# Attention feeding a hard-swish MLP: head-pair tokens in 128 by 3 plus shared blocks of 64, in place of 112 by 4

## The chip, the cores and the metric

The kernel runs on one core of a Trainium2 chip. The metric is device time in microseconds (us), the median of several runs of the whole program. The engines are TensorE (PE in the profile, with its weight loads as PEld), VectorE (DVE), ScalarE (ACT), GpSimd (POOL) and SyncE (SP). SP issues nearly all the DMAs.

## The reference

Two parts, one after the other. All inputs and the output are float32.

```python
# q, k, v: (8 batches, 12 heads, 448 tokens, 64); g_q, g_k: (64,)
def rmsnorm(x, g):
    return x / np.sqrt(np.mean(x * x, axis=-1, keepdims=True) + 1e-06) * g
q_n, k_n = rmsnorm(q, g_q), rmsnorm(k, g_k)
scores = q_n @ k_n.T / sqrt(64)              # per batch and head, 448 x 448
attn = softmax(scores)                       # the row maximum is subtracted first
a = attn @ v
x = a, as (8 * 448, 12 * 64)                 # 3584 x 768
h = x @ w_in                                 # w_in 768 x 2048
g = h * clip(h + 3, 0, 6) / 6
out = g @ w_out                              # w_out 2048 x 768, out 3584 x 768
```

## The kernel before

The work unit of attention is the head pair, two heads of one batch. There are 48 of them, P = 0 to 47, six per batch. The 448 tokens of a head pair are mapped as 112 partitions by T = 4, token p * 4 + t. For each head pair:

- `load` (L376) issues three DMAs on SP: q, k and v of both heads, 224 KB each, in rows of 1 KB.
- `prep` (L388) squares q and k on ACT or POOL, sums the squares per token on VectorE (L406), takes ln and exp on ACT (L411, L414) for the reciprocal root, multiplies q and k by it into bfloat16 `qks` (L423, POOL, and VectorE for the first head pair), and casts v into `va` (L345, L347, L351), which has a column of ones beside each 64 values.
- `trans` (L446) turns `qks` so that the two heads' 64 features lie on 128 partitions and tokens run along the free axis: the tile `T`, 448 columns of queries and 448 of keys. For the first 13 head pairs TensorE transposes (L475) and VectorE or ACT copies; from the 14th on it is a DMA transpose on SP (L451). The keys take the gains and the scale along (L460, L462, L484, L486).
- `score` (L498) multiplies, for a block t of keys, each head's 64 feature rows with all 448 queries. The two heads use the upper and the lower 64 rows of TensorE side by side (L506). ACT takes the exponential of both heads at once, 896 columns, from PSUM to `eT` (L515). No maximum is subtracted, since the normed scores are bounded.
- `av` (L520) uses `eT` as the stationary operand, 128 columns of queries at a time, and streams the 65 columns of `va` (L527): 8 matmuls per key block, 32 per head pair, summed over the four blocks in the PSUM tile `X`. The 65th column is the softmax sum.
- `finish` (L533) takes the reciprocal of the sums (L539), multiplies (L542) and turns the result into `xT`, features on partitions: by TensorE for batches 0 and 1 (L558), by DMA transpose from batch 2 on (L549).

The MLP works per batch: `h_group` (L567) makes 128 of the 2048 hidden features for 448 tokens in six matmuls (L579), ACT makes the clamp's lower half (L586, a Relu with 1/6 folded in), and VectorE does the upper half and the product with h into `gT` (L589). `y_group` (L597) makes 128 tokens of the output for a pair of batches, 2 x 16 matmuls of 384 columns (L610), copied by ACT or VectorE (L347, L349) and stored by one to several DMAs, since a block of 128 tokens cuts the 112-partition map at changing places. The weights are loaded and cast to bfloat16 by four DMAs each on POOL's queue (L645, L650).

The order is written out. Every step is an operation of a `Plan` with reads, writes and a wished time; the list `ORDER` gives the sequence of all operations, and each engine executes its own in that sequence. The table `WAY` names the operations that use the second or third of several possible engines. So each engine's queue is fixed, and an engine waits at the head of its queue. PSUM is divided into two score tiles S, one tile X for AV (and for some scores) and two banks M for the MLP. Head pairs are grouped for scores: one key block at a time for the first six, two at a time to head pair 23, and from 24 on three blocks (the third in X) with the fourth joined to the first of the next head pair. MLP matmuls lie between these groups.

Of the kernel before, what the change touches and what calls it, by code (L numbers as in the profile page):

```python
# [8 lines left out]
FP32 = mybir.dt.float32  # L9
# [3 lines left out]
A_MIN = mybir.AluOpType.min  # L13
LN = mybir.ActivationFunctionType.Ln
# [7 lines left out]
WAY = {53: 1, 63: 2, 67: 1, 68: 1, 69: 1, 78: 1, 83: 1, 84: 1, 95: 1, 101: 1, 126: 1, 132: 2, 157: 1,  # L22
    163: 1, 183: 1, 188: 1, 225: 1, 231: 1, 233: 1, 245: 1, 250: 1, 256: 1, 276: 1, 358: 1, 365: 1, 377: 1,
    388: 1, 400: 1, 424: 2, 429: 1, 446: 1, 453: 1, 458: 1, 460: 1, 487: 1, 500: 1, 505: 1, 516: 1, 518: 1,
    533: 1, 625: 1, 636: 1, 676: 1, 683: 2, 709: 2, 714: 1, 728: 1, 729: 1, 755: 1, 761: 2, 766: 1, 793: 1,
    798: 1, 821: 1, 892: 1, 899: 2, 925: 2, 930: 1, 945: 1, 951: 2, 977: 2, 1003: 2, 1008: 1, 1023: 1,
    1029: 1, 1034: 1, 1061: 1, 1097: 1, 1134: 1, 1148: 1, 1182: 2, 1206: 1, 1212: 1, 1226: 1, 1251: 1,
    1257: 2, 1263: 1, 1398: 1, 1413: 1, 1420: 2, 1426: 1, 1440: 1, 1447: 1, 1453: 1, 1464: 1, 1465: 1,
    1491: 1, 1515: 1, 1516: 1, 1522: 1, 1549: 1, 1555: 1, 1579: 1, 1615: 1, 1620: 1, 1652: 1, 1673: 1,
    1693: 1, 1700: 1, 1706: 1, 1718: 1, 1724: 2, 1744: 1, 1751: 2, 1757: 1, 1781: 1, 1795: 1, 1832: 1,  # L30
    1893: 1, 1921: 1, 1932: 1, 1938: 1, 1958: 1, 1971: 1, 1979: 1, 1980: 1, 1986: 1, 1992: 1, 2057: 1,
    2062: 1, 2093: 1, 2098: 1, 2125: 1, 2145: 1, 2162: 1, 2169: 1}


class Plan:
# [51 lines left out]
    8, 9, 20, 13, 21, 22, 15, 23, 11, 24, 28, 10, 25, 19, 29, 53, 26, 12, 30, 27, 14, 54, 31, 16, 55, 32, 33,  # L87
    34, 17, 58, 35, 56, 36, 83, 37, 92, 38, 78, 59, 39, 60, 40, 57, 62, 41, 18, 69, 42, 43, 44, 61, 45, 93,
    68, 66, 46, 73, 47, 67, 64, 123, 48, 101, 70, 49, 50, 74, 122, 65, 75, 71, 63, 77, 104, 72, 217, 102, 84,
    105, 76, 81, 85, 154, 51, 103, 112, 94, 124, 82, 79, 52, 86, 114, 80, 113, 153, 126, 115, 110, 87, 95,  # L90
    155, 135, 88, 111, 96, 91, 89, 136, 106, 116, 184, 117, 107, 133, 97, 118, 90, 143, 119, 185, 156, 108,
    134, 132, 120, 186, 144, 109, 141, 121, 248, 142, 145, 146, 166, 98, 1, 157, 164, 147, 167, 158, 148, 99,
    165, 174, 163, 149, 215, 137, 150, 159, 172, 100, 125, 387, 138, 151, 175, 127, 0, 139, 216, 173, 218,
    140, 187, 152, 195, 128, 197, 188, 129, 196, 176, 177, 178, 198, 130, 179, 189, 203, 160, 204, 205, 131,
    246, 180, 168, 181, 190, 206, 161, 169, 170, 247, 182, 171, 191, 183, 162, 228, 385, 226, 229, 207, 194,
    208, 386, 201, 227, 199, 192, 209, 416, 202, 210, 200, 236, 211, 234, 225, 212, 237, 230, 414, 219, 213,
    249, 259, 214, 231, 6, 220, 238, 260, 239, 193, 235, 445, 267, 2, 221, 232, 240, 222, 268, 241, 257, 223,
    242, 233, 243, 415, 258, 250, 261, 244, 262, 245, 265, 256, 251, 277, 266, 278, 224, 269, 279, 280, 281,
# [109 lines left out]
def kernel(  # L208
# [11 lines left out]
    nc = tc.nc  # L220

    B, H, S, D = q.shape
    DM, DFF = moe_w_in.shape
    NPAIR = H // 2
    NP = B * NPAIR
    T = 4
    TP = S // T
    NKT = DM // 128
    NFT = DFF // 128
    E1 = D + 1  # L230
    HALF = DM // 2
    S2 = 2 * S
# [58 lines left out]
    for t in va_r:  # L291
        nc.gpsimd.memset(t[:, :, :, D:E1], 1.0)
# [481 lines left out]
```

## Time and profile before

| | |
|---|---|
| time, median of 3 runs | 432.89 us (431.69 to 434.04) |
| the profiled execution | 432.39 us |
| its span, first to last instruction | 430.6 us |
| TensorE busy | 415.5 us, 97% of the span |
| ACT busy | 296.6 us, 69% |
| VectorE busy | 220.7 us, 51% |
| POOL busy | 171.8 us, 40% |
| mean granted TensorE clock | 0.988 |
| DMA packets | 94418, of which 53156 under 512 bytes |
| HBM read, written | 45.61 MB, 11.01 MB |

The profile is one execution. In its forty slices each digit is the busy share in tenths of a slice of 10.8 us. In groups and in the timeline a line names the line of the kernel, the engine, the operation, the tile written and those read, the shape and the count. A matmul's duration includes its way through the array, so matmuls in a row overlap and start-to-start distances give their price. In a list of waits the numbers are total us, times and the longest one.

### The profile page before, as it was taken

How to read it: one execution, taken by the hardware profiler on the slowest of the kernel's cores; microseconds unless marked ns; L12 is line 12 of the kernel's file. 1: busy time of each engine (PE TensorE's matmuls, PEld its weight loads, DVE VectorE, ACT ScalarE, POOL GpSimd, SP SyncE). 2: the span in 40 equal slices, each digit the busy share in tenths (PEclk: the TensorE clock that was granted, in tenths of full speed). 3: DMA queues.
4: the chain of work that ended last, by engine and by line, in shares of the span. 5: the costliest groups of instructions: out<-in, count | busy, mean ns of one | idle time of the engine just before them, and what ended most of it. 6: DMA issues, size and time to landing. Idle time of an engine off the chain costs nothing.

```text
span 430.6 us, 9771 instructions
## 1 busy us (share of the span) xinstructions
PE 415.5 (97%) x3874; PEld 238.0 (55%) x3874; DVE 220.7 (51%) x405; ACT 296.6 (69%) x535; POOL 171.8 (40%) x188
## 2 busy tenths in 40 slices
PE   7678999999999999999999999999999999999996
PEld 7445555555555555555555555555555555655554
DVE  5665677557688865565556344434424332143211
ACT  4988899898998888968856978575575546222221
POOL 2897865876647867345434350312200000000000
PEclk9968999999999999999999999999999999999999
DMA  8999999499979999657564755262313221021113
GB/s 211 257 246 253 238 241 248 103 227 219 223 203 216 208 220 231 177 145 184 149 158 118 202 147 130 65 117 70 78 32 84 49 59 49 12 73 38 37 39 110
DMA packets 94418, 63.13 MB, mean 147 GB/s; under 512 B 53156, under 2 KB 90916, under 8 KB 94372
## 3 DMA queue, kind: packets, MB, share of 16 engines
q1 hardware_dynamic: 88736, 55.88, 53.5%
q0 software_dynamic: 5248, 6.29, 8.3%
q8 instruction: 30, 0.49, 0.5%
q10 hardware_dynamic: 388, 0.34, 0.3%
q14 instruction: 16, 0.13, 0.1%
HBM read 45.61 MB, written 11.01 MB: 132 GB/s over the span
## 4 chain that ended last, share of the span: by engine, by line
PE 90%; DMA 5%; ACT 2%; DVE 1%; issue 1%; SPq 1%
PE M L579 32%; PE M L610 29%; PE X L527 11%; PE S L506 9%; PE S L610 5%; DMA qk<-in_q_dram 3%; DMA vf<-in_v_dram 2%; PE X L579 1%; ACT eT L515 1%; PE X L506 1%; PE S L579 1%; PE X L610 1%; DVE ssq L406 1%; SPq L384 1%; DVE gT L589 0%
## 5 line engine op out<-in xcount | busy, mean ns | idle before, releaser
L515 ACT ACTIVATE eT<-S 112x896 bf16<-112x896 f32 x168 | 148.0, 918 | 16.1 <-PE S L506 15.6
L579 PE MATMUL M<-xT,w_in_sb 128*128 128x448 bf16 x714 | 153.2, 353 | 0.6 <-ACT xT L347 0.3
L610 PE MATMUL M<-w_out_sb,gT 128*128 128x384 bf16 x752 | 135.9, 326 | 0.0
L589 DVE SCALAR_TENSOR_TENSOR gT<-ts,M 128x448 bf16<-128x448 f32 x119 | 73.4, 619 | 102.6 <-ACT ts L586 102.4
L423 POOL TENSOR_TENSOR qks<-qk,rs 112x512 bf16<-112x512 f32 x94 | 96.2, 1044 | 61.8 <-DMA T<-qks 33.5
L610 PEld LDWEIGHTS <-gT 128*128 128x128 bf16 x912 | 84.8, 98 | 62.1 <-issue 9.9
L586 ACT ACTIVATE ts<-M 128x448 f32<-128x448 f32 x119 | 64.8, 547 | 61.4 <-PE M L579 60.2
L579 PEld LDWEIGHTS <-w_in_sb 128*128 128x128 bf16 x768 | 69.9, 98 | 65.4 <-issue 10.8
L399 POOL TENSOR_TENSOR sq<-qk 112x512 f32<-112x512 f32 x56 | 57.7, 1040 | 44.8 <-DMA qk<-in_k_dram 18.3
L527 PEld LDWEIGHTS <-eT 112*128 112x128 bf16 x1536 | 57.8, 99 | 19.0 <-issue 8.7
L406 DVE TENSOR_REDUCE ssq<-sq 112x16 f32<-112x1024 f32 (+1 forms) x50 | 58.0, 1172 | 15.9 <-ACT sq L397 11.6
L527 PE MATMUL X<-va,eT 112*128 112x65 bf16 x1536 | 62.8, 196 | 1.0 <-DVE xT L349 0.6
L506 PE MATMUL S<-T 64*128 64x448 bf16 x336 | 48.5, 363 | 4.2 <-ACT eT L515 2.1
L542 DVE TENSOR_TENSOR xn<-X,rd 112x512 bf16<-112x512 f32 x48 | 33.2, 691 | 1.8 <-DVE rd L539 0.2
L351 POOL CAST va<-vf 112x512 bf16<-112x512 f32 x20 | 12.8, 638 | 45.3 <-PE X L527 42.8
L506 PEld LDWEIGHTS <-T 64*128 64x128 bf16 x384 | 13.1, 94 | 29.8 <-issue 22.5
L397 ACT ACTIVATE sq<-qk 112x512 f32<-112x512 f32 x40 | 24.8, 627 | 4.6 <-DMA qk<-in_k_dram 3.1
L347 ACT COPY y<-M 128x384 f32<-128x384 f32 x26 | 12.5, 481 | 18.7 <-PE M L610 18.4
L539 DVE RECIPROCAL rd<-X 112x8 f32<-112x8 f32 x48 | 9.8, 204 | 30.1 <-PE X L527 29.8
L349 DVE COPY y<-M 128x384 f32<-128x384 f32 x21 | 11.7, 555 | 22.8 <-PE M L610 22.6
L515 ACT ACTIVATE eT<-X 112x896 bf16<-112x896 f32 x24 | 22.1, 923 | 0.0
L610 PE MATMUL S<-w_out_sb,gT 128*128 128x384 bf16 (+1 forms) x128 | 21.8, 316 | 0.0
(56 smaller groups left out, 178.6 us busy)
## 6 DMA issues: line engine op xcount, KB each, us to landing
qk<-in_q_dram SPq DMA_DIRECT2D x48, 224.0 KB, 4.4
qk<-in_k_dram SPq DMA_DIRECT2D x48, 224.0 KB, 3.9
vf<-in_v_dram SPq DMA_DIRECT2D x48, 224.0 KB, 4.4
w_in_sb<-in_moe_w_in_dram POOLq DMA_DIRECT2D x4, 768.0 KB, 14.5
w_out_sb<-in_moe_w_out_dram POOLq DMA_DIRECT2D x4, 768.0 KB, 15.1
out_dram<-y SPq DMA_DIRECT2D x7, 336.0 KB, 2.8
out_dram<-y SPq DMA_DIRECT2D x8, 288.0 KB, 2.7
out_dram<-y SPq DMA_DIRECT2D x8, 240.0 KB, 2.8
```

What stands on the lines that cost most here:

```text
L397: em(nc.scalar.square(out=sq[:, i], in_=x))
L399: em(nc.gpsimd.tensor_tensor(out=sq[:, i], in0=x, in1=x, op=A_MULT))
L406: em(nc.vector.tensor_reduce(out=ssq[:, s].rearrange("p i n -> p (i n)"), in_=sq[:, s].rearrange("p i (n d) -> p (i n) d", d=D), axis=AX_X ...
L423: em((nc.vector if e == DVE else nc.gpsimd).tensor_tensor(out=qks[:, i].rearrange("p t h d -> p h t d"), in0=qk[:, i].rearrange("p h (t d) ...
L506: em(nc.tensor.matmul(out=ps[:, a, 0:S], lhsT=qkT[r, S + t * TP:S + t * TP + 128], rhs=qkT[r, 0:S], start=True, stop=True))
L515: em(nc.scalar.activation(out=eT[:, t, 0:S2].rearrange("p (a s) -> p a s", a=2), in_=ps[0:TP, :, 0:S], func=EXP, bias=0.0, scale=1.0))
L527: em(nc.tensor.matmul(out=X_ps[:, a, i * E1:(i + 1) * E1], lhsT=eT[:, t, c:c + 128], rhs=va[:, a, t, :], start=(t == 0 and i == 0), stop=( ...
L542: em(nc.vector.tensor_tensor(out=xn[:].rearrange("p i a d -> p a i d"), in0=xv[:, :, :, 0:D], in1=rd[:].unsqueeze(3).to_broadcast([TP, 2, ...
L579: em(nc.tensor.matmul(out=ps[:, 0:S], lhsT=w_in_sb[:, kt, f * 128:(f + 1) * 128], rhs=xT[:, kt, :], start=(kt == 0), stop=(kt == NKT - 1)))
L586: em(nc.scalar.activation(out=ts[:], in_=ps[:, 0:S], func=RELU, bias=0.5, scale=1.0 / 6.0))
L589: em(nc.vector.scalar_tensor_tensor(out=gT[:, f, e * S:(e + 1) * S], in0=ts[:], scalar=1.0, in1=ps[:, 0:S], op0=A_MIN, op1=A_MULT))
L610: em(nc.tensor.matmul(out=ps[:, 0:nc0], lhsT=gT[:, f, i * 128:(i + 1) * 128], rhs=w_out_sb[:, f, c0:c0 + nc0], start=(f == 0), stop=(f == ...
```

## The change

The token map becomes 128 partitions by 3, token p * 3 + t, for the first 384 tokens of a head, and the last 64 tokens (RT) are in blocks of their own, shared by the head pairs 2m and 2m+1:

- The last 64 queries of the even and the odd head pair share one block of 128 columns, so that in `T`, which now holds two head pairs, the even one's 448 queries end where the odd one's begin.
- The last 64 keys of a head pair's two heads lie on a diagonal: head 0 in rows 0 to 63 and columns 0 to 63, head 1 in the others, zeros elsewhere. One matmul over all 128 rows gives both heads' scores for them, with keys of head 0 on partitions 0 to 63 and of head 1 on 64 to 127 (`rest`). Its exponential has 448 columns for both heads.
- The values of these keys lie on a diagonal too, `vb`, 130 columns: one AV matmul serves both heads.

Per head pair there are three key blocks with 896-column exponentials and one of 448; 24 AV matmuls of 65 columns and 4 of 130. Loads are three DMAs of 192 KB per head pair, in rows of 768 bytes, and per two head pairs six of 32 KB in rows of 256 bytes. `prep` scales q and k on POOL or, in the first batch, on VectorE in six instructions of one 64-element group each. The DMA transposes have nine blocks of 128 for the even head pair and six for the odd, in place of eight of 112 for each.

Two things change beside. The clamp of the MLP can run on ACT (Relu of h + 3) or on VectorE (h held between -3 and 3), with the other half in the product and the sixth in the output copy. The score groups are one key block at a time to head pair 5, two and one to head pair 17, then three at once; no group joins two head pairs. `ORDER` and `WAY` are new throughout. The core of the diff:

```diff
-    T = 4
-    TP = S // T
+    T = 3
+    TP = 128
+    RT = S - T * TP
...
+    KE, KR, QE, QR, QO, KO = 0, 3 * TP, 5 * TP, 8 * TP, 9 * TP, 12 * TP
...
-    NQK, NV, NSQ, NRS, NQS, NVA, NT, NE, NXN, NXT, NTS, NY = 5, 5, 2, 4, 3, 4, 4, 2, 2, 2, 2, 3
+    NQK, NV, NVR, NSQ, NRS, NQS, NVA, NVB, NT, NE, NXN, NXT, NTS, NY = 5, 5, 2, 2, 4, 2, 4, 3, 2, 2, 2, 2, 2, 3
...
-    qks_r = ring(NQS, [TP, 2, T, 2, D], BF16, "qks")
-    va_r = ring(NVA, [TP, 2, T, E1], BF16, "va")
-    T_r = ring(NT, [128, S2 + PAD], BF16, "T")
-    eT_r = ring(NE, [TP, T, S2 + PAD], BF16, "eT")
+    qke_r = ring(NQS, [TP, 9, 2, D], BF16, "qke")
+    qko_r = ring(NQS, [TP, 6, 2, D], BF16, "qko")
+    va_r = ring(NVA, [TP, 2 * T, E1], BF16, "va")
+    vb_r = ring(NVB, [TP, 2, 2, E1], BF16, "vb")
+    T_r = ring(NT, [128, 15 * TP], BF16, "T")
+    eT_r = ring(NE, [TP, T, S2 + 2 * PAD], BF16, "eT")
+    eR_r = ring(NE, [TP, S + 2 * PAD], BF16, "eR")
...
+            for n in range(2):
+                r = slice(n * RT, n * RT + RT)
+                if c == "R":
+                    rows = src[b, four, T * TP:S, :].rearrange("(o h) r d -> o r h d", o=2)[n]
+                    dst = qk[r, FULL + 2 * D:FULL + 4 * D].rearrange("p (h d) -> p h d", h=2)
+                else:
+                    rows = src[b, four, T * TP:S, :].rearrange("(o h) r d -> h r o d", o=2)[n]
...
+                if e == DVE:
+                    for h in range(2):
+                        for t in range(T):
+                            c = c0 + h * T + t
+                            em(nc.vector.tensor_scalar(
+                                qks[:, b0 + t, h], x[:, h, t], rs[:, c:c + 1], None, A_MULT, A_ADD,
+                                accum_out=junk_t[:]))
...
+    def rest(P, want):
+        ps, res = sbank()
+
+        def f_sr(_):
+            qkT, k0, q0 = T_r[P // 2 % NT], KR + P % 2 * TP, queries(P)
+            em(nc.tensor.matmul(
+                out=ps[:, 0, 0:S], lhsT=qkT[:, k0:k0 + TP], rhs=qkT[:, q0:q0 + S], start=True, stop=True))
+
+        def f_er(_):
+            em(nc.scalar.activation(
+                out=eR_r[P % NE][:, PAD:PAD + S], in_=ps[:, 0, 0:S], func=EXP, bias=0.0, scale=1.0))
+        plan.add(pe(0.19), want, f_sr, sorted(treads(P, ["KR"])), [res])
+        plan.add([act(S)], want, f_er, [res], [("e", P % NE, T)])
...
         def f_av(_):
-            for a in range(2):
-                for i in range(T):
-                    c = a * S + i * TP
+            for i, c in enumerate(columns(P)):
+                for h in range(2 if t < T else 1):
+                    c0 = PAD + h * S + c
+                    o = (i % 2 * 2 + h) * E1
                     em(nc.tensor.matmul(
-                        out=X_ps[:, a, i * E1:(i + 1) * E1], lhsT=eT[:, t, c:c + 128],
-                        rhs=va[:, a, t, :], start=(t == 0 and i == 0), stop=(t == T - 1),
-                        skip_group_check=True))
+                        out=X_ps[:, i // 2, o:o + (E1 if t < T else 2 * E1)],
+                        lhsT=eT[:, t, c0:c0 + TP] if t < T else eR[:, c0:c0 + TP],
+                        rhs=va[:, h * T + t, :] if t < T else vb[:, P % 2].rearrange("p h e -> p (h e)"),
+                        start=(t == 0 and h == 0 and i % 2 == 0), stop=(t == T), skip_group_check=True))
...
-        def f_r(_):
-            em(nc.scalar.activation(out=ts[:], in_=ps[:, 0:S], func=RELU, bias=0.5, scale=1.0 / 6.0))
+        def f_r(eng):
+            made_by.append(eng)
+            if eng == ACT:
+                em(nc.scalar.activation(out=ts[:], in_=ps[:, 0:S], func=RELU, bias=3.0, scale=1.0))
+            else:
+                em(nc.vector.tensor_scalar(ts[:], ps[:, 0:S], -3.0, 3.0, A_MAX, A_MIN))
...
-        plan.add([act(S)], want + dt, f_r, [res], [("ts", key)])
+        plan.add([act(S), dve(S)], want + dt, f_r, [res], [("ts", key)])
...
-        if P < NPAIR:
+        if P < NG0:
             groups = [([(P, t, False)], w + t * step) for t in range(T)]
...
-            groups = [([(P, t, False), (P, t + 1, False)], w + t * step) for t in (0, 2)]
+            groups = [([(P, 0, False), (P, 1, False)], w), ([(P, 2, False)], w + 2 * step)]
...
-        elif P % 2 == 0:
-            groups = [([(P, 0, False), (P, 1, False), (P, 2, True)], w),
-                      ([(P, 3, False), (P + 1, 0, False)], w + G2 * step)]
-            aw, fw = w + AE * step, w + FE * step
-        else:
-            groups = [([(P, 1, False), (P, 2, False), (P, 3, True)], w + G3 * step)]
-            aw, fw = w + AO * step, w + FO * step
+        else:
+            groups = [([(P, 0, False), (P, 1, False), (P, 2, True)], w)]
+            aw, fw = w + AE * step, w + FE * step
```

## The prediction, made before the changed kernel was run

> **What bounds the kernel now.** The page came first: its busy times, then the forty slices.
>
> ```profile
> PE 415.5 (97%) x3874; PEld 238.0 (55%) x3874; DVE 220.7 (51%) x405; ACT 296.6 (69%) x535; POOL 171.8 (40%) x188
> ...
> PE   7678999999999999999999999999999999999996
> ...
> ACT  4988899898998888968856978575575546222221
> ...
> PEclk9968999999999999999999999999999999999999
> DMA  8999999499979999657564755262313221021113
> ```
>
> TensorE is the engine that is never free, except in the first four slices (43 us). There the clock drops too (6 and 8 tenths), ACT runs at 8 to 9 tenths and the DMA engines at 8 to 9. So there are two kernels in one: a start-up paced by ACT, DMA and their latencies, and a rest paced by TensorE. Busy time by stage puts the border near 46 us, where the last xT copy of batch 0 lets the first hidden-layer matmuls of L579 run dense:
>
> ```profile
> core 0: us, PE busy (x) PEld busy (x) DVE busy (x) ACT busy (x) POOL busy (x), PEclk, DMA share, GB/s
> 0.00:46.40 46.40, 35.41 (x472) 25.48 (x473) 27.36 (x57) 36.20 (x69) 33.71 (x46) 0.89 1.08 242
> 46.40:76.00 29.60, 29.00 (x302) 16.14 (x302) 21.06 (x37) 27.14 (x53) 18.80 (x21) 1.00 1.12 239
> 76.00:427.00 351.00, 351.00 (x3102) 196.34 (x3100) 172.31 (x313) 232.93 (x414) 119.29 (x123) 1.00 0.53 127
> ```
>
> From 76 us on TensorE is busy 351.00 of 351.00 us: only fewer or shorter matmuls help there. Their prices come from the timeline of TensorE:
>
> ```profile
> 205.33 2.76 PE L610 MATMUL M<-w_out_sb,gT 128*128 128x384 bf16 x16
> 208.02 0.55 PE L506 MATMUL S<-T 64*128 64x448 bf16 x4
> 208.41 0.35 PE L506 MATMUL X<-T 64*128 64x448 bf16 x2
> 208.69 0.82 PE L610 MATMUL M<-w_out_sb,gT 128*128 128x384 bf16 x4
> 209.35 1.30 PE L579 MATMUL M<-xT,w_in_sb 128*128 128x448 bf16 x6
> 210.59 0.55 PE L506 MATMUL S<-T 64*128 64x448 bf16 x4
> 211.07 1.47 PE L610 MATMUL M<-w_out_sb,gT 128*128 128x384 bf16 x8
> 212.38 0.41 PE L527 MATMUL X<-va,eT 112*128 112x65 bf16 x8
> 212.62 0.81 PE L610 MATMUL M<-w_out_sb,gT 128*128 128x384 bf16 x4
> ```
>
> Read start to start. A 384-column matmul takes 162 ns (eight take 1.30 in the chain of waits), a 448-column one 189 (six take 1.14). Eight of AV (L527): 0.24, so 30.5 ns. A score matmul uses 64 rows, two heads side by side: one pair of them costs 189, like one full matmul. But three pairs take 0.67 (208.02 to 208.69), two take 0.48 (210.59 to 211.07): 0.10 more than 0.57 and 0.38. And the first score comes 0.09 late: from 205.33 to 208.02 are 2.69, sixteen matmuls take 2.60. So entering and leaving a run of row-split matmuls costs 0.19 us.
>
> With these prices, 49 ns per 112-column transpose (four take 0.20) and 57 per 128-column warm-up matmul (sixty take 3.4), the whole instruction order sums to 404.4 us of TensorE; the first matmul starts at 1.0 and the last at 426.9, so 21.5 us are idle or half-clock, of which 18 before 46.4. From 46.4 on it sums to 377.0 against 380.4 on the clock.
>
> **TensorE, part by part.** *Scores*: four pairs per head pair become three plus one undivided 128-row matmul for both heads' last 64 keys: 4 x 189 as before. What changes is the number of runs: 88 in the old order, 67 in the new (a head pair from 18 on has one run; before, two head pairs had three). 21 x 0.19 = 4.0 us less. The new matmul is in the shape of L579 and opens no run of its own. *AV*: 1536 matmuls of 65 columns become 1152 of 65 and 192 of 130. No row has 130 columns: at least 57 ns (the 128-column warm-ups), at most 61 (two of 65). From 384 to 448 columns are 27 ns, 0.42 a column, so 30.5 + 65 x 0.42 = 58. 1536 x 30.5 = 46.8; 1152 x 30.5 + 192 x 58 = 46.3: 0.5 less (0.8 to 0.1). *Transposes*: 152 of 112 columns become 147 of 128; 7.4 to 8.2 us, 0.7 more. Together the order is some 4 us shorter.
>
> Where the 4 us lie decides. Summed up to the xT transposes of batch 0's last head pair, the old order holds 27.4 us and the new 24.9: 2.5 us vanish from a stage in which TensorE waits anyway, at no gain. What remains behind that point falls from 377.0 to 375.4: **1.6 us** gained, as long as the stage stays dense.
>
> **ACT.** Per head pair four exponentials of 896 become three and one of 448. In a row they start 0.81 apart (2.53 us for three with 0.92 latency); one of 448 takes 547 ns against 918, so 0.37 less: 0.37 x 48 = 18 us of busy time. Of the 128 clamps (L586, 547 ns) 74 go from ACT to VectorE. After 46.4 us TensorE's stream covers ACT, so there this brings nothing but room. In the start-up it counts: from the first exponential (12.5) to that last xT copy (46.4) ACT issues 29.3 us of work in 33.9; the new order has 27.6 for the same stretch. **1.7 us** less. The 1.1 us that TensorE idles between 46.4 and the first L610 come from late exponentials and clamps; I take half, **0.6**, as gone.
>
> **VectorE and POOL.** Clamps cost VectorE some 620 ns each (like gT, L589), 46 us; what hides them is that VectorE waits 107.8 us for ACT's clamps now. If that cover were gone, a bank of M would be held 0.07 us longer per group, 5 us over 74, and L579's next group would wait. In the start-up, scaling by POOL (1044 ns per 512 elements) goes for many blocks to VectorE as six 64-element instructions, each between a reciprocal (204 ns) and a 512-element copy (678 plus 82): six take 1.2 to 4.5 us; near the small row, about 1.3. Up to the sixth xn there are 48 of them, 10 us on an engine that is busy 27 of 46: it fills to about 37, still under ACT. POOL has nearly the same work until then. These are priced at nothing, with up to 4 us in the range.
>
> **DMA and SP.** The same bytes, in other packets: per two head pairs 1344 of 1 KB become 1536 of 768 bytes and 768 of 256. Loads are 288 instead of 144, 0.31 to 0.50 us of SP each, with the transposes queued behind. In the start-up the engines are full (share 1.08; 256 GB/s from 10 to 20 us, over 16 engines 64 ns per 1 KB packet). Six head pairs were 4032 packets, 16.1 us; 4608 of 768 bytes by bytes are 13.8. The 2304 of 256 bytes cost 16 ns each by bytes and 64 if a packet is a packet: 2.3 to 9.2 us. The nearest row is that of the transposes' 256-byte packets, 24 ns in the trace's packet records: 3.5. So 13.8 + 3.5 - 16.1 = **1.2 us** more (0 to 6.9). Query rows of head pair 0 are only the ninth load (4 us later in SP's queue), but its keys are prepared meanwhile, and the first exponential at 12.5 waited for ACT, not for scores; nothing. The Trainium skill speaks against this edit: "DMA: Bandwidth & Descriptors", Specifications, wants at least 512 bytes for line rate, and "Why small descriptors are slow (HBM only)" puts the loss of 256-byte ones at 27%. By that, an estimate, 0.6 us would stand in place of 1.2; no row here shows a 256-byte load from memory.
>
> **Sum.** The profiled execution took 432.39 (span 430.6). Less 1.7, plus 1.2, less 0.6, less 1.6 = 429.7. The median of the runs lies 0.5 above that execution: **430.2**.
>
> **Rivals.** *Slower: late loads in the start-up.* Place: head pairs 1 to 5, before 46 us. POOL reaches the first w_in transfer after 3.9 us of its own work instead of 10.3, so about 10 us earlier than at 19.3. Where that queue ran beside the loads (25 to 35 us) their rate halved, from some 1250 to 581 KB per 5 us. Six us at half rate are 3 us; with the packet price midway, 4, loads are 7 us late: 432.9 - 1.7 - 0.6 - 1.6 + 7 = 436 (433 to 439). Slower by over 0.5% begins at 6.1 us. For it: the full DMA slices. Against: from 10 us to 46.4 engines wait only some 2 us for loads.
>
> *DMA in 80 to 165 us.* Share 0.94; by the packet records after 76 us (1 KB 59 ns, 256 bytes 24, so 768 some 47) a head pair would cost 0.36 more for its loads (672 x 59 against 768 x 47 + 384 x 24, over 16 engines) and 0.19 for 128 more transposed rows of 24 ns, 15 pairs 8 us; 5 are idle, so 3 to 8 land on TensorE if the lead of T over its scores, some 9 us, is used up by then: 433 to 438. First the wait
>
> ```profile
> POOL qks L423 <- DMA T<-qks: 33.5, 9, 12.4
> ```
>
> grows, then TensorE waits for T.
>
> *No change.* The shortened order is hidden and ACT's gain eaten by VectorE's small instructions: 431 to 434.
>
> *Better.* In 20 to 40 us the clock is 0.75: 10 us at half rate. The skill's "TensorE: Matmul & The Clock Gate", Part 1, expects that after about 3.4 idle us; here the longest pause was 1.9. TensorE is busy some 8 of those 10 us, so an order that escapes it gains up to 4 us more: 425 to 428.
>
> **How the numbers follow.** Forecast 0.48 (427 to 432.5), late loads 0.22, DMA later 0.12, no change 0.08, better 0.10. Within 0.5%, about what a measurement can tell from no change, is 430.7 to 435.1. The forecast's 0.48 gives 0.34 to faster and 0.14 to same (its middle lies just past the border); late loads and DMA give 0.30 to slower, 0.04 to same; no change 0.08 to same; better 0.10 to faster. The range 425 to 439 leaves out the worst of the loads and the best of the clock.
>
> **What would show it.** Right: TensorE back to back from about 74 us, the rest of the order some 1.6 us shorter, 0.19 per run still; last xT of batch 0 copied at 45 to 46.5. Wrong: that copy after 48, TensorE waits for T, xT or weights after 76 us, a 130-column AV over 61 ns, or a score run that the undivided matmul lengthens.

## The result, and the profile after

The changed kernel takes 465.13 us (median of 4 runs, 462.85 to 466.53) against 432.44 for the kernel before beside it: ratio 1.075, 95% interval 1.069 to 1.080. The prediction was 430.2 (425 to 439). The profiled execution is the one of 462.85, its span 461.1.

From the page, busy times, and TensorE's and the DMA engines' rows of the forty slices (now 11.5 us each):

```profile
PE 423.9 (92%) x3629; PEld 246.4 (53%) x3629; DVE 279.5 (61%) x644; ACT 253.6 (55%) x486; POOL 161.8 (35%) x264
...
PE   8486899999889897999898999999999999999996
...
DMA  6888999757866767677789767755144411120112
```

TensorE is no longer full after the start-up: there are 8s and a 7 as far as slice 22. The DMA engines, which the prediction took to be the pressed resource, are emptier than before in most of the first slices. Busy time by stage, in the columns shown before; the last line is that of the kernel before for the same stretch as the line above it:

```profile
core 0: us, PE busy (x) PEld busy (x) DVE busy (x) ACT busy (x) POOL busy (x), PEclk, DMA share, GB/s
0.00:46.40 46.40, 32.69 (x339) 23.01 (x340) 31.33 (x139) 28.46 (x58) 24.41 (x57) 0.83 0.80 171
46.40:76.00 29.60, 28.20 (x266) 16.96 (x264) 21.41 (x47) 21.37 (x46) 20.23 (x30) 0.92 1.13 231
76.00:427.00 351.00, 332.59 (x2835) 187.66 (x2833) 220.26 (x448) 198.53 (x373) 117.12 (x179) 1.00 0.58 134
85.00:260.00 175.00, 156.78 (x1388) 87.40 (x1386) 115.59 (x240) 113.08 (x229) 89.20 (x132) 0.99 0.72 168
```

```profile
85.00:260.00 175.00, 175.00 (x1699) 95.95 (x1697) 111.06 (x200) 145.18 (x272) 98.72 (x101) 1.00 0.79 190
```

Up to 46.4 us the DMA share is 0.80 where it was 1.08, and from 85 to 260 us TensorE idles 18.2 of 175 us; before, it idled none of them. The last xT copy of batch 0 ends at 55.2 us (46.4 before). So of the 30.5 us by which the span grew, 8.8 arise ahead of that point and 21.7 behind it.

It is not TensorE's own work. Its timeline in a dense stretch, start to start:

```profile
300.79 0.55 PE L670 MATMUL S<-T 64*128 64x448 bf16 x4
301.18 0.35 PE L670 MATMUL X<-T 64*128 64x448 bf16 x2
301.47 1.31 PE L769 MATMUL M<-xT,w_in_sb 128*128 128x448 bf16 x6
302.61 0.35 PE L690 MATMUL S<-T 128*128 128x448 bf16 x1
302.80 1.46 PE L806 MATMUL M<-w_out_sb,gT 128*128 128x384 bf16 x8
```

Three score pairs take 0.68 to the start of the next matmul (priced 0.67), six of L769 1.14 (1.14), the undivided matmul of L690 0.19 (0.19). Set against the matmuls of the order in these prices, TensorE loses some 25 us between 80 and 260 us, where the kernel before loses some 1.

Where does the loss come from? Two pieces of the chain of waits in that stage (start, duration, what; SPq is SP's queue issuing a DMA, DMA the time from an issue to its landing):

```profile
168.38 0.63 SPq L457
169.02 0.05 issue
169.07 0.59 SPq L830
169.66 0.04 issue
169.70 0.60 SPq L457
170.30 0.04 issue
170.35 2.16 DMA qk<-in_k_dram
172.51 0.07 issue
172.58 1.05 POOL sq L488
...
177.65 3.19 DMA qk<-in_q_dram
...
180.92 0.10 ACT sq L486
...
181.46 2.52 ACT eT L680 x3
183.97 0.05 issue
184.02 1.01 PE X L715 x22
```

SP issues one DMA after the other with 0.04 to 0.05 us between, the small loads of L457 among them, and the square on POOL waits for the last. The second piece shows the way to TensorE: a square on ACT waits for its load too, the exponentials (eT) stand behind it in ACT's queue, and TensorE's AV matmuls (X) wait for them. The lists of waits say the same (us in all, times, longest), first the kernel before, then the changed one:

```profile
POOL sq L399 <- DMA qk<-in_q_dram: 13.3, 7, 4.5
```

```profile
POOL sq L488 <- DMA qk<-in_q_dram: 26.2, 10, 7.9
```

Between 85 and 260 us ACT's squares wait 19.9 us for loads of q and k, and before they waited 0.6.

What one issue occupies of SP is in the trace of each line (duration in ns: min/median/max). First the loads of the kernel before, then the small loads of the changed one:

```profile
L384 SPq DMA_DIRECT2D qk<-in_q_dram x48: 312/416/1269, 0.7 to 259.8; - x48
```

```profile
L457 SPq DMA_DIRECT2D qk<-in_q_dram x48: 595/607/912, 2.3 to 290.2; - x48
```

A load of 32 KB in 128 packets holds SP longer than one of 224 KB in 224 packets. All issues of SP together, added up from the trace, take 280 us of the span instead of 181.

### The profile page after: what moved, and what is told of

It reads as the page before. It is cut to its first block, busy times and chain, and to the rows that moved or that the text cites. A ratio compares the mean times of both kernels' runs of the same rounds, so it can differ in the third digit from the quotient of the medians.

```text
span 461.1 us, 9700 instructions
## 1 busy us (share of the span) xinstructions
PE 423.9 (92%) x3629; PEld 246.4 (53%) x3629; DVE 279.5 (61%) x644; ACT 253.6 (55%) x486; POOL 161.8 (35%) x264
## 4 chain that ended last, share of the span: by engine, by line
PE 48%; DMA 7%; SPq 4%; DVE 3%; POOL 2%; ACT 1%; issue 1%; ACTq 0%; POOLq 0%; DVEq 0%
PE M L806 17%; PE M L769 15%; PE X L715 4%; PE S L806 4%; DMA qk<-in_k_dram 3%; DMA qk<-in_q_dram 2%; PE S L670 2%; PE X L769 1%; SPq L457 1%; SPq L602 1%; POOL sq L488 1%; PE S L769 1%; ACT eT L680 1%; DMA T<-qko 1%; SPq L438 1%
## 5 line engine op out<-in xcount | busy, mean ns | idle before, releaser
L769 PE MATMUL M<-xT,w_in_sb 128*128 128x448 bf16 x714 | 156.8, 355 | 5.7 <-DVE gT L786 2.3
L680 ACT ACTIVATE eT<-S 128x896 bf16<-128x896 f32 x114 | 102.0, 915 | 41.3 <-PE S L670 41.1
L769 PEld LDWEIGHTS <-w_in_sb 128*128 128x128 bf16 x768 | 71.3, 98 | 73.3 <-issue 19.1
L786 DVE SCALAR_TENSOR_TENSOR gT<-ts,M 128x448 bf16<-128x448 f32 x119 | 73.5, 619 | 33.5 <-ACT ts L780 30.9
L495 DVE TENSOR_REDUCE ssq<-sq 128x12 f32<-128x768 f32 (+4 forms) x51 | 52.3, 1027 | 33.1 <-POOL sq L488 24.5
L488 POOL TENSOR_TENSOR sq<-qk 128x384 f32<-128x384 f32 (+2 forms) x49 | 44.7, 917 | 64.6 <-DMA qk<-in_q_dram 26.2
L715 PEld LDWEIGHTS <-eT 128*128 128x128 bf16 x1152 | 45.8, 99 | 22.5 <-issue 7.0
L782 DVE TENSOR_SCALAR ts<-M 128x448 f32<-128x448 f32 x73 | 45.2, 621 | 18.4 <-PE M L769 18.1
L715 PE MATMUL X<-va,eT 128*128 128x65 bf16 x1152 | 49.5, 196 | 6.2 <-ACT eT L680 3.9
L528 POOL TENSOR_TENSOR qke<-qk,rs 128x384 bf16<-128x384 f32 x45 | 36.8, 825 | 26.5 <-ACT rs L503 20.4
L780 ACT ACTIVATE ts<-M 128x448 f32<-128x448 f32 x46 | 25.0, 546 | 38.2 <-PE M L769 37.3
L528 POOL TENSOR_TENSOR qko<-qk,rs 128x384 bf16<-128x384 f32 x44 | 35.6, 827 | 17.5 <-DMA T<-qko 8.4
L732 DVE TENSOR_TENSOR xn<-X,rd 128x512 bf16<-128x512 f32 x48 | 33.2, 691 | 5.1 <-DMA xT<-xn 3.2
L819 DVE TENSOR_SCALAR y<-M 128x384 f32<-128x384 f32 x27 | 14.9, 553 | 26.7 <-PE M L806 26.6
L670 PEld LDWEIGHTS <-T 64*128 64x128 bf16 x288 | 11.1, 94 | 26.9 <-issue 19.9
```

What stands on the lines that cost most here:

```text
L488: em(nc.gpsimd.tensor_tensor(out=o, in0=x, in1=x, op=A_MULT))
L495: em(nc.vector.tensor_reduce(out=ssq[:, c0:c1], in_=sq[:, c0 * D:c1 * D].rearrange("p (n d) -> p n d", d=D), axis=AX_X, op=A_ADD))
L528: em(nc.gpsimd.tensor_tensor(out=qks[:, b0:b0 + T].rearrange("p t h d -> p h t d"), in0=x, in1=rs[:, c0:c0 + 2 * T].rearrange("p (h t) -> ...
L670: em(nc.tensor.matmul(out=ps[:, a, 0:S], lhsT=qkT[r, k0:k0 + TP], rhs=qkT[r, q0:q0 + S], start=True, stop=True))
L680: em(nc.scalar.activation(out=eT[:, t, PAD:PAD + S2].rearrange("p (a s) -> p a s", a=2), in_=ps[:, :, 0:S], func=EXP, bias=0.0, scale=1.0))
L715: em(nc.tensor.matmul(out=X_ps[:, i // 2, o:o + (E1 if t < T else 2 * E1)], lhsT=eT[:, t, c0:c0 + TP] if t < T else eR[:, c0:c0 + TP], rhs ...
```

## The experiments

Three theories at first. **Q**: what the small loads cost is the time in which their queue issues them, with large loads and transposes behind. **P**: their 256-byte packets hold the DMA engines. **O**: the new written order has too little lead whatever the loads cost. In runs without an interval the time is one execution, beside 430 to 434 for the kernel before. The share of SP's issue in a stage and the us at half clock are added up from the trace.

**1. Small loads left out from head pair 10 on.** The last 64 rows of later heads are then not loaded, and old rows stand in their place.

```diff
-                def fn(_, dst=dst, rows=rows):
-                    em(nc.sync.dma_start(out=dst, in_=rows))
+                def fn(_, dst=dst, rows=rows, P=P):
+                    if P < 10:
+                        em(nc.sync.dma_start(out=dst, in_=rows))
```

> The changed kernel without the 256-byte-row loads from head pair 10 on (114 of 144 are left out; later head pairs use what lies in the buffers, so that part of the result is stale). Theory Q (SP's queue: 144 more load instructions of 0.61 us each fill it): the time falls from 465 to 430-440, SP's issue share between 100 and 260 us falls from 0.9 to about 0.65. Theory P (small packets hold the DMA engines): falls as much. Theory O (the new fixed order is too tight in itself): stays above 455.

441.28 us; TensorE idles 1.9 us from 85 to 260. So O falls for this stage: the same order runs dense once the loads are gone. 9 to 10 us over the kernel before remain, all in the start-up: the last xT copy of batch 0 ends at 56.2, 9.8 us later than there.

**2. All 288 loads, the small ones with 8 rows instead of 64 from head pair 10 on.** Again not all rows are loaded.

```diff
+                    if P >= 10:
+                        dst, rows = dst[0:8], rows[0:8]
```

> The changed kernel with all 288 loads, but from head pair 10 on the small ones move 8 rows instead of 64, so 16 packets of 256 bytes instead of 128 (the rest of the rows is stale). Theory Q, if an issue costs per instruction: 455-466, SP still at 0.61 us per small load. Theory Q, if it costs per packet: SP's duration falls under 0.3 us and the time to 435-445. Theory P: 430-440 with SP's durations unchanged. Theory O: above 455 as in the run without the loads.

440.46 us. A small load now takes 0.36 to 0.41 us of SP (median), all issues 241 us, and TensorE is dense again, though SP still issues for 0.79 of the stage:

```profile
85.00:260.00 175.00, 172.90 (x1552) 98.27 (x1548) 130.46 (x267) 128.24 (x258) 95.20 (x141) 1.00 0.75 173
```

Number of instructions alone is not the cost, then; but both the issue time and the packets fell, so Q and P stay.

**3 and 4. The kernel before, with 144 added loads of 64 rows by two 256-byte packets into a tile that nobody reads; on SP, then on ACT's queue.**

```diff
...
+                d = dummy_r[ndummy[0] % len(dummy_r)]
+                ndummy[0] += 1
+                em(nc.sync.dma_start(out=d[:], in_=src[b, hs, 0:64].rearrange("h r d -> r h d")))
```

(nc.scalar in place of nc.sync in the fourth.)

> The kernel before with 144 loads added on SP, one behind each of its own, of 64 rows x 2 x 256 bytes into a scratch tile that nobody reads. Theory Q: SP's issue share between 100 and 160 us goes from 0.8 to over 0.95 and the time rises by 10 to 30 us, 443-463. Theory P: rises about as much. Theory O: 432-436.

> The same 144 added loads, issued on ACT's queue instead of SP's: same packets, same bytes. Theory Q: clearly less than with SP, 433-442 (ACT pays 0.4 to 0.6 us for each, and is busy 69%). Theory P: the same time as with SP. Theory O: 432-436.

480.86 and 468.87 us, both above what Q expected (443 to 463, and 433 to 442), and not alike, where P had them alike. The old order with added loads on SP shows the loss of the new one and more:

```profile
85.00:260.00 175.00, 153.08 (x1448) 82.06 (x1445) 96.26 (x171) 127.09 (x235) 89.57 (x92) 0.97 0.79 179
```

An added load took 602 ns of SP, and in the fourth run 603 of ACT, where TensorE waits for exponentials instead (L512 for eT, 15.5 us). So Q was right that the issue holds its engine, and wrong that ACT had room for it. In the line above the DMA share is 0.79, as in this stage without the added loads.

**5 and 6. The changed kernel, small loads on POOL's, then on ACT's queue.**

```diff
-                    em(nc.sync.dma_start(out=dst, in_=rows))
+                    em(nc.gpsimd.dma_start(out=dst, in_=rows))
```

> The changed kernel with its 144 small loads (64 rows by two 256-byte packets) issued by POOL instead of SP; transfers, order and all else as they were. Theory Q (what the small loads cost is the time that SP takes to issue them, 0.60 us each, with the large loads and the transposes queued behind): SP's issue falls from 280 to about 188 us, the idle time of TensorE in 100 to 260 us goes (25 to under 6 us), and the time is 433 to 450 us, the upper part if POOL's squares now come late. Theory P (the 256-byte packets hold the DMA engines): packets and bytes are the same, so the time stays at 460 to 467. Theory O (the new order is too tight): 460 to 467 too.

> The changed kernel with its 144 small loads issued by ACT instead of SP. Theory Q: ACT gets some 90 us of issue on top of 254 us busy; the loss moves to ACT, where exponentials queue behind the issues, 440 to 458 us, and SP's issue is about 188 us. Theory P: 460 to 467, and nothing depends on which engine issues.

459.49 and 464.17 us: outside what Q expected (433 to 450, and 440 to 458), the first half a us below P's 460 to 467, the second inside it. By the time alone these two speak for P. SP's issue fell as it should, to 181 and 189 us, and the idle time of TensorE from 85 to 260 us from 18.2 to 9.7 and 14.9; but the other engine takes 0.60 to 0.63 us a load now, with its own work behind: POOL is busy for 247 us, ACT for 256 plus 92 of issue. The start-up got slower too (last xT copy of batch 0 at 60.7 and 59.0). Another queue was no way out here. How much of what stays is the issue time on that engine and how much its place in that engine's order, these two don't tell.

**7. Small loads left out from head pair 2 on** (tiles of rest rows hold a constant). A fourth theory, **W**, is that the first w_in transfer, which the new order issues at 7.8 us instead of 19.3, delays the start-up.

```diff
...
-                def fn(_, dst=dst, rows=rows):
-                    em(nc.sync.dma_start(out=dst, in_=rows))
+                def fn(_, dst=dst, rows=rows, P=P):
+                    if P < 2:
+                        em(nc.sync.dma_start(out=dst, in_=rows))
```

> The changed kernel with the small loads left out from head pair 2 on (6 of 144 are left; the tiles of rest rows hold a constant, so the last 64 rows of most heads are not computed). It asks what the 9 us are that were left over the kernel before when they were left out from head pair 10 on. If the small loads of the first pairs cause them (theory Q in the start-up): the first dense stretch of TensorE begins at 46 to 48 us and the time is 429 to 434 us. If it is the place of the first transfer of w_in in the new order, with larger transposes (theory W): the start stays late, at 52 to 54 us, and the time is 437 to 441.

438.18 us, and the last xT copy of batch 0 at 53.2: small loads are some 2 us of the start-up, not more, and both numbers lie where W had them. How far single executions differ shows in the first two runs, which share the changed kernel's loads up to head pair 9: this copy ends at 56.2 and 54.9 there, 55.2 in the changed kernel.

**8. The kernel before, with 72 added loads of 64 rows by four packets**: bytes and packets of the third run in half the instructions.

```diff
...
+                if ndummy[0] % 2 == 0:
+                    d = dummy_r[ndummy[0] // 2 % len(dummy_r)]
+                    h4 = slice(4 * (j // 2), 4 * (j // 2) + 4)
+                    em(nc.sync.dma_start(out=d[:], in_=src[b, h4, 0:64].rearrange("h r d -> r h d")))
```

> The kernel before with 72 added loads on SP of 64 rows by four packets of 256 bytes each: the packets and the bytes of the run that cost 49.7 us with 144 loads of two packets a row, in half as many instructions. If the issue costs by the instruction (Q1): 0.60 us each, 43 us of SP, and the time is 445 to 458 us. If it costs by the packet (Q2): 1.2 us each, 87 us of SP, and 475 to 482. Theory P (the packets on the DMA engines): 475 to 482 as well, but with each issue at about 0.60 us.

448.79 us instead of 480.86. One issue took 0.60 to 0.62 us, as with two packets a row. P falls as the main cause: the same packets and bytes cost 17.6 us over the kernel before beside it, where they cost 49.7. Q holds in its form Q1, a price for each instruction.

**9 to 12. The start-up: VectorE's scaling in one instruction (theory S), and w_in later (W).** The ninth is the changed kernel with

```diff
-                if e == DVE:
-                    for h in range(2):
-                        for t in range(T):
...
-                else:
-                    em(nc.gpsimd.tensor_tensor(
+                em((nc.vector if e == DVE else nc.gpsimd).tensor_tensor(
...
```

and the same for the two query rests. The tenth has this on the seventh run's kernel, the eleventh has there the first w_in transfer moved from place 59 of `ORDER` to place 154, the twelfth both. As in the seventh, rest rows of most heads are not computed in these three.

> The changed kernel with VectorE's scaling of a block of keys or queries in one instruction of 384 elements (as POOL does it) instead of six of 64 elements and their six accumulator reads; nothing else changes. In the start-up 48 small pieces at 0.32 us each (15 us of VectorE) become 8 instructions of some 0.70 (6 us). Theory S (these pieces lie on the chain of the start-up and are what is left of the loss once the small loads are gone): the first dense stretch of TensorE begins 3 to 6 us earlier, and the time is 457 to 462 from 465, since the loads' loss after 85 us stays. Theory W (the early w_in transfer): no change, 463 to 467.

> The run that left the small loads out from head pair 2 on (438.2 us), with VectorE's scaling in one instruction instead of six. Theory S: 431 to 434. Theory W: 437 to 439. With both at work: 434 to 437.

> The run that left the small loads out from head pair 2 on (438.2 us), with the first transfer of w_in moved in the written order from place 59 to place 154, just before the second one; its matmuls begin after 46 us. Theory W: the loads of 10 to 15 us keep the memory to themselves, 431 to 435. Theory S: 437 to 440.

> Both edits together on the run without the small loads from head pair 2 on. If the three costs (small loads, small pieces of VectorE, early w_in) are all that the prediction missed, this is what it forecast: 427 to 431 us, with the first dense stretch of TensorE at 45 to 47 us. If it stays above 434, a cost in the start-up is still unnamed.

461.44, 442.51, 438.64 and 435.76 us. The last xT copy of batch 0 ends at 52.8 us (55.2 in the changed kernel), then 57.2, 53.7 and 50.4 (53.2 in the seventh). W alone brings nothing. S alone is worth 2.4 us in the full kernel and minus 4 without the loads, where half-clock stretches make up 30.7 us before 60 instead of 20.5. Only both together help, 2.8 us: beside S, the later w_in is worth 6.8 us (57.2 to 50.4), so the two don't add. What the prediction forecast is not reached by taking away all three costs, so one was still unnamed. Two candidates were left: the clock (theory **C**), since the changed kernel has 20.5 us at half clock before 60 us and the kernel before 10.2; and the order itself.

**13 to 16. Fewer loads with the same bytes, and the clock.** From batch 1 on, the rest rows of a whole batch are loaded together into tiles of their own: 74 small loads instead of 144, in the same 256-byte packets; the squares of rest rows become instructions of their own.

```diff
...
+                if b == 0 or j == 0:
+                    hh = four if b == 0 else slice(0, 2 * NPAIR)
+                    m0, m1 = (j, j + 2) if b == 0 else (0, 6)
+                    if c != "R":
+                        todo = [(tile_[r, m0:m1], src[b, hh, T * TP:S, :].rearrange("(o h) r d -> h r o d", h=2)[n])]
...
```

The fourteenth adds the single scaling instruction. The fifteenth adds to that, and the sixteenth to the kernel before (there after the first three groups):

```diff
+            if P < 6 and t < T:
+                for _ in range(10):
+                    em(nc.tensor.matmul(
+                        out=X_ps[:, 0, 0:128], lhsT=zero_t[:], rhs=zero_t[:], start=False, stop=False,
+                        skip_group_check=True))
```

> The changed kernel with the rest rows of a whole batch loaded together from batch 1 on (tiles of their own, 74 small loads instead of 144; the same bytes in the same 256-byte packets), and with the squares of rest rows in instructions of their own. The result is the full one. Theory Q (a load costs its issue): SP's issue falls by some 42 us to about 240, TensorE is dense from 100 us on as in the run with few rows, and the time is 439 to 445 us. Theory P (the packets): 455 to 466.

> The same, with VectorE's scaling in one instruction instead of six. Theory Q and S: 435 to 441. If only the half-clock stretches decide the start-up (theory C), it follows their number: near 436 with one stretch before 60 us, near 441 with two.

> The same, with ten matmuls of zeros (128 columns, 57 ns each) added into the AV accumulator after every group of AV of head pairs 0 to 5 (they add nothing to the sums), so that TensorE pauses less in the start-up. Theory C: fewer us at half clock before 60 us (10 instead of 20), and 430 to 436. If the clock is not what costs: the same as without, or up to 5 us slower, since the zeros stand in TensorE's queue.

> The kernel before with the same ten matmuls of zeros after the first three AV groups of head pairs 0 to 5. Theory C: its one half-clock stretch (24.7 to 35.0 us) gets shorter or goes, 426 to 431 us. If the clock costs nothing there, since ACT and the loads set the pace: 431 to 436.

441.08, 440.13, 450.95 and 435.92 us. The thirteenth is the test of Q in the changed kernel itself, with the full result: 24 of the 33 us are back (in the profiled executions 21.8 of 30.5), with every byte and every 256-byte packet still moved:

```profile
85.00:260.00 175.00, 171.73 (x1541) 97.40 (x1540) 129.47 (x266) 128.41 (x271) 97.66 (x157) 1.00 0.85 186
```

The DMA share is higher than in the changed kernel (0.85 against 0.72), TensorE's idle time 3.3 us against 18.2. This edit also fetches rest rows a batch ahead, which could help by itself; but the second run kept every load in its place, and the added loads of the eighth were waited for by nobody, and both say the same. C found no support: with the zeros the kernel before had full clock from 5.9 us to the end and was no faster (435.92, beside 433.89 without). But the 180 zero matmuls take TensorE themselves, some 10 us at 57 ns, and the last xT copy came at 49.9 instead of 46.4, so a gain by the clock could be hidden behind their cost. In the changed kernel the zeros did not keep the clock up (20.5 us at half clock before 60 us) and the run became 11 us longer. So the clock's part in the start-up was not told apart.

**17 and 18. The order of the start-up.** The first exponential of the changed kernel begins at 20.36 us, 7.9 later than before (12.47), and from there to the last xT copy of batch 0 it takes 34.8 us, before 33.9. So by subtraction most of the start-up's loss lies ahead of the first exponential. POOL's timeline of the changed kernel there (in brackets the idle time before it, and what ended it):

```profile
12.90 0.83 POOL L528 TENSOR_TENSOR qke<-qk,rs 128x384 bf16<-128x384 f32 x1 [0.90 <-ACT rs L503]
17.60 0.51 POOL L399 CAST va<-vf 128x384 bf16<-128x384 f32 x1 [3.88 <-DMA vf<-in_v_dram]
18.19 0.86 POOL L554 TENSOR_TENSOR qke<-qk,rs 64x128 bf16<-64x128 f32 x2
```

The rest keys of head pair 0 (L554), without which its scores can't start, are queued behind a copy of v that waits for its load; that load is the fifteenth in SP's order, loads of head pairs 1 to 3 go ahead of it, and those of 1 and 2 ahead of head pair 0's queries too. And it lands late: SP issues it at 9.25, and the copy can start only at 17.6. The first w_in transfer is under way from 7.8 to 17.8 us. Of the loads whose landing the trace has, those issued ahead of 8 us land 2.2 to 3.2 us after their issue, those from 8.6 to 13.4 us 5.9 to 8.2 us after it; in the eleventh run, with that transfer moved, loads issued in this stretch take 3.5 to 4.8 us. So POOL's 3.9 us of waiting belong to the early w_in transfer as well as to the order of the queues. ACT likewise has squares of head pair 3 ahead of the first exponentials. In the seventeenth run (on the fourteenth's kernel) the first 300 of the 2466 steps in `ORDER` are in a new sequence, by a list scheduler with SP's measured issue times; the beginning of it:

```diff
-    8, 19, 32, 20, 33, 34, 10, 35, 25, 36, 40, 14, 37, 11, 38, 65, 15, 39, 68, 9, 41, 12, 69, 42, 70, 43, 21,
...
+    9, 32, 40, 41, 10, 33, 42, 11, 43, 34, 8, 44, 35, 14, 45, 36, 12, 46, 37, 13, 66, 47, 38, 15, 65, 71, 48,
...
```

The eighteenth is by the same scheduler, with other rules for SP's loads and the w_in transfers.

> The kernel with the rest rows of a batch loaded together and single scaling instructions (440.1 us), with the first 300 of its 2466 steps put in another order, by a small list scheduler that takes a load for 0.5 to 0.6 us of SP and 2 us of latency: loads, squares and scalings of head pair 0 first, copies of v behind the rest keys, w_in from 20 us on. Nothing else changes, and the result is the full one. Theory O' (the order ahead of the first exponential): the first exponential at 11 to 14 us instead of 20.5, the last xT copy of batch 0 at 45 to 48 instead of 53.2, and 431 to 435 us. If the start-up is held by the amount of work of ACT, VectorE and the loads instead: the last xT copy stays after 51, and 437 to 442.

> The run with the new order of the first 300 steps (439.5 us), but with SP's loads of head pairs 0 to 5 strictly pair by pair ahead of any load of the next batch, and the first three w_in transfers set at 23, 31 and 38 us of the schedule instead of 20, 23 and 29. Theory O' (the order of loads, w_in and POOL's work is all of the start-up's loss): the fifth and sixth xT copies at 38 to 40 and 43 to 46 us instead of 47.4 and 52.6, and 430 to 435 us. If a cost other than the order holds the sixth copy, it stays after 50, and the time is 437 to 441.

439.48 us (ratio to before 1.020, interval 1.013 to 1.026) and 440.3 (1.022, 1.015 to 1.028). Half of what O' expected came true: the first exponential at 11.1 and 11.7 us and the fourth xT copy at 33.6 in both, where the kernel before has 36.5 and the changed one 46.2. Then it is lost again: the fifth ends at 47.4 and 45.3, the sixth at 52.6 and 53.2. The sixth copy after 50 us and both times lie where the two expectations had the rival: a start-up held by its amount of work, or by a cost other than the order. In the seventeenth run the chain of waits names rest rows of v that were issued behind loads of the next batch and beside three w_in transfers:

```profile
30.17 11.85 DMA vr<-in_v_dram
```

In the eighteenth, where these were moved, it is the w_in transfer itself that the first hidden-layer matmul needs and that is issued at 41.8:

```profile
PE M L643 <- DMA w_in_sb<-in_moe_w_in_dram: 3.6, 1, 3.6
```

So it is shown that the written order, the place of w_in in it included, holds the first exponential back by 8 us or more, and that this can be had back as far as the fourth copy. That a start-up can be written which keeps it to the end is not shown; neither run beats the kernel before. What the last 9 us of the 33 come from stays open: the written order, the w_in transfers beside the loads, VectorE's pieces, the clock and the amount of work each have some evidence, and no run has the time back.

## Why the prediction was wrong

**The step that failed: "DMA and SP".** It asked what the loads cost the DMA engines, counted packets, and came to 1.2 us. It did note 288 issues "0.31 to 0.50 us of SP each, with the transposes queued behind", and then gave them no price and no place. Both halves were off. The new loads take 0.607 us each, more than the 0.50 that I took as the end of the range from rows of loads seven times their size. And the queue was never looked at by stage: in the trace of before SP issues for 0.68 of the time between 85 and 260 us, 0.81 between 100 and 130. Against the issue time, the runs with all loads on SP's queue line up:

| kernel | SP issue in all, us | its share, 85 to 260 us | TensorE idle there, us | time, us |
|---|---|---|---|---|
| before | 181 | 0.68 | 0.0 | 432.4 |
| small loads left out from 10 on | 205 | 0.61 | 1.9 | 441.3 |
| 8 rows each | 241 | 0.79 | 2.1 | 440.5 |
| loaded by the batch | 245 | 0.78 | 3.3 | 441.1 |
| before, 72 added | 262 | 0.84 | 5.3 | 448.8 |
| changed | 280 | 0.87 | 18.2 | 465.1 |
| before, 144 added | 287 | 0.86 | 21.9 | 480.9 |

Up to a share of 0.8 the stage is all but dense; at 0.87 a tenth of it is gone. In shorter stretches the share says less: in the thirteenth run SP is at 0.86 to 0.93 from 110 to 210 us, and TensorE idles 1.3 us there; in the changed kernel it is at 0.89 to 0.92 from 110 to 260 us, and TensorE idles 16.1. The fourth, fifth and sixth runs, where another engine issues, lie beside this table: SP's share is 0.58 to 0.60, and TensorE idles 9.7 to 14.9 us. Issuing fewer loads gave back 24 of the 33 us. The Trainium skill has the mechanism: by "Perfetto Trace Analysis", DMA Instruction — HWDGE (DVE, Sync), an issue holds its sequencer until all its descriptors are generated. The traces agree that the time is the issuing engine's (602 ns on SP, 603 on ACT) and that it is a price of its own beside the transfer; that it should grow with the number of descriptors they show only between 8 and 64 rows.

**Second: "Query rows of head pair 0 are only the ninth load ...; nothing."** The first exponential came 7.9 us later. I argued that it had waited for ACT in the kernel before. That was true there and said nothing of the new order, in which POOL waits for a load ahead of the rest keys. The order per engine was there to be read, loads of head pairs 1 to 3 ahead of head pair 0's and all; I counted the place of the load and did not follow who was queued behind it, nor that the first w_in transfer would run beside these loads. How much of the time this step cost is not shown: in the seventeenth run the first exponential came at 11.1 us and the last xT copy still at 52.6.

**TensorE, part by part: right.** The prices held (0.68 for a run of three pairs, 0.19 for the undivided matmul, 56 ns for 130 columns of AV in the trace, the median, priced 58), and the order is as much shorter as said. It is worth nothing here, since the stage behind 46.4 us didn't stay dense, which was the condition named. The prediction's own first sign of being wrong, that copy after 48, came true with 55.2.

**ACT: not seen.** From the first exponential to the last xT copy of batch 0 it was to be 1.7 us less than 33.9; it is 34.8. With VectorE's single instructions (ninth run) it is 32.5 (20.3 to 52.8), near the 32.2 that the prediction comes to. That fits a lighter load of ACT that VectorE's small instructions took, a term priced at nothing that would be 2.4 us, inside the 4 that the range held for it. It isn't shown: the ninth run also has less half clock before 60 us (13.7 us instead of 20.5), and without the small loads the same edit lost 4 us.

**The rivals.** *Late loads in the start-up* had the sign and about the size of the first part, and one half of its mechanism is in the trace: beside the early w_in transfer loads landed 5.9 to 8.2 us after their issue instead of 2.2 to 3.2. Moving that transfer brought no time by itself (eleventh run) and 6.8 us beside the single scaling instruction (435.76 against 442.51), so its part stays open. The other half, small packets that fill the engines, isn't there: the DMA share up to 46.4 us is 0.80, not over 1.08 (1.16 only from 12 to 16 us, beside that transfer). *DMA in 80 to 165 us* had nearly the place of the second part, again by packets; its sign, a longer wait for T, didn't show (POOL's wait for T of 33.5 us fell to 17.6: 8.4 and 5.5 at L528, 3.7 at L554). From 85 to 260 us the engines had room: share 0.72, and 0.85 in the thirteenth run, in which TensorE is nearly dense. *Better*, by the clock, found no support in the sixteenth run, which had full clock only at the price of the zeros.

The Trainium skill's 27% for 256-byte packets ("DMA: Bandwidth & Descriptors", "Why small descriptors are slow (HBM only)") agrees with the packet records about as far as they go: up to 46.4 us 256-byte packets took 18.9 ns on average and 768-byte ones 42.5, a quarter less by the byte. (The 0.6 us of the prediction added 27% to the time; a rate 27% lower makes it 0.9.) But at these prices the loads of six head pairs take 15.0 us of the 16 engines, where the prediction had 17.3 and the loads before 16.1, so this is not what cost the time. The range missed because all slower cases had the DMA engines as their limit, none the queue in front of them.

## What to carry to other kernels

Before a change adds DMAs, sum the issue time of their queue by stage, in the trace of before, and see what share of each stage it holds already: a load costs its queue mostly by the instruction and little by its bytes (0.60 us here for 32 KB, 0.42 for 224 KB). Here a share of 0.8 over 175 us was all but free, and 0.87 cost a tenth of the time. Joining small transfers into fewer ones gave back most of the loss; handing them to an engine that computes gave back little, since that engine then paid 0.60 to 0.63 us for each. And where queues are written out by hand, follow, for the first work item, which load each engine waits for, what large transfer runs beside that load, and what stands behind it: here POOL stood for 3.9 us at a copy whose load landed late, with all scores behind it.

## What the runs showed of the hardware that was not expected

- A load's issue took 0.60 to 0.62 us (medians) for 64 rows of two, four and (by the batch) six 256-byte packets alike, on SP and on ACT (0.62 to 0.63 on POOL); 0.41 to 0.45 (0.31 at the least) for 112 rows of two 1 KB packets; 0.53 (0.37) for 128 rows of two 768-byte packets; 0.36 to 0.41 (0.27) for 8 rows of two 256-byte ones. So at 64 rows it follows neither bytes nor packets.
- Full clock in the start-up did not pay for the matmuls that kept it up: with ten zero matmuls behind each of the first three AV groups of head pairs 0 to 5 the kernel before ran at full clock from 5.9 us on and took 435.9 us, beside 433.9.
- A small load that usually lands after 3 us took up to 8.2 beside one 768 KB transfer on another queue, and 11.9 beside three.
